# Two-layer MLP chain with banded attention: the norm's factors taken by token and spread by DMA, and a planner that shakes its due times at random

## The chip, the cores and the metric

One core of one Trainium2 chip runs the whole program. The metric is device microseconds of one execution; the times shown are medians of runs, and the profile is that of one execution.

## What is computed

The program chains three blocks. All arrays are fp32.

```python
scores = scale * q @ k.T + bias, kept where the key is global (8) or within the last 96
x1 = softmax(scores) @ v                       # (2, 8, 768, 64) -> 1536 tokens x 512
x2 = np.maximum(x1 @ w_in, 0.0) ** 2 @ w_out   # 512 -> 2048 -> 512
rms = np.sqrt(np.mean(x2 * x2, axis=-1, keepdims=True) + 1e-06)
xn = x2 / rms * rms_g
out = (silu(xn @ w_gate) * (xn @ w_val)) @ w_out2   # 512 -> 1536 -> 512
```

## The kernel before

Tokens are cut into four chunks `c` of 384 columns. Activations lie transposed: features on the 128 partitions, tokens along the row, in tiles `xh`, `xl` (a high and a low part of each fp32 number). A product of two such split operands is three matmuls (`mm3`, lines 385 to 387) into one PSUM bank `b0` to `b7`.

The stages follow each other on TensorE (PE):
- **Attention** for the four chunks (tiles `ps`, `p`, `tb`, `pt`, `av`), with the first four of the sixteen feature blocks of the first MLP for chunks 0 to 2 laid between (`first`). Weights come by DMA into `wraw` and are unpacked on ACT (L416, L418), DVE (L420), and split into `M` (L375, L376).
- **First MLP**, middle blocks: `squared` and `outs`, a seven-product scheme over pairs of chunks (`quad`), sums into `y`.
- **First MLP, last four blocks, and the norm** (`rest`, `norm_sum`, `norm`): after chunk c's last `first`, ACT squares its four `y` rows, DVE adds them into `ns`, one matmul with a matrix of ones (L610) sums over the partitions and leaves the sum in all 128 rows, ACT takes the root (L613), and DVE takes the reciprocal in three pieces of 128 columns (L616). `norm` multiplies `y` by this `ns` and by `rms_g` (`fin`, L637), subtracts pairs of blocks, and splits the results into `xh`, `xl` and `ar`.
- **Second MLP**: `gated` (gate products, SiLU, value products) and `final`, which writes the output.

The order of all of this is not written by hand. `Plan` holds every operation with its engine, an assumed duration, and its dependences; `forward` plays a list schedule in which each engine takes the ready operation with the earliest due time, `backward` derives new due times from the result, and `solve` repeats this for seven values of a lead that attention gets, and keeps the due times with the earliest end. The program is then emitted in order of planned start, and every engine executes its instructions in that order. Where PE would stand idle in the plan between 1 and 60 us, or between 330 and 400 us, `emit` puts small matmuls with ones (L1362, *fillers* below) whose result nobody reads.

The planner's costs for a transfer are these: it holds SP for 0.45 us or more (`DMA`), and an operation on another engine that needs it may start 2.6 us after that (`LAT["SP"]`); an operation on the same engine that needs it may start at once, since `SAME["SP"]` is 0.

Of the kernel before, what the change touches and what calls it, by code (L numbers as in the profile page):

```python
# [3 lines left out]

# [1 line left out]

# [6 lines left out]
F32 = mybir.dt.float32  # L13
# [6 lines left out]
P = 128  # L20
# [56 lines left out]
class Plan:  # L77
# [33 lines left out]
    def solve(self):  # L111
        for o in reversed(self.ops):
            for q in o.succ:
                o.due = min(o.due, q.due - o.dur - (o.lat if q.eng != o.eng else SAME[o.eng]))
        best = None
        for lead in LEADS:
            if best is not None:
                for o, due in zip(self.ops, best[1]):
                    o.due = due - (lead if o in self.ahead else 0.0)
            for _ in range(ROUNDS):  # L120
                self.forward()
                end = max(o.end for o in self.ops)
# [146 lines left out]
class Mlp:  # L269
# [5 lines left out]

    def __init__(self, nc, plan, tl, main, late, psm, psl, srcs, gcol, epst, ones, ident, out):
        self.nc, self.plan, self.tl, self.out = nc, plan, tl, out
        self.gcol, self.epst, self.ones, self.ident, self.srcs = gcol, epst, ones, ident, srcs  # L280
        for k in range(KD):
# [8 lines left out]
        for n in range(2):  # L290
            tl.define(f"wraw{n}", main, [P, 1026], I32)
            tl.define(f"p5{n}", late, [P, CH], F32)
            tl.define(f"ns{n}", late, [P, CH], F32)
        for n in range(3):
            tl.define(f"wbits{n}", main, [P, 512], F32)
            tl.define(f"H{n}", late, [P, 512], F32R)
        for n in range(5):
            tl.define(f"ra{n}", main if n < 3 else late, [P, CH], F32)
        for n in range(4):
            tl.define(f"nq{n}", late, [P, CH], F32)  # L300
        tl.define("ar", late, [P, 24 * CH], F32R)
        for n in range(8):
            tl.define(f"b{n}", psm if n < 4 else psl, [P, 512], F32)
        self.nraw = self.nbits = self.nload = self.nact = self.nra = self.np5 = self.nnq = 0
# [234 lines left out]
            self.relu2(lambda f=f: self.tl(f"b{banks[f]}")[:, :CH], [("b", banks[f])], act[f, c % 2])  # L539
        return act  # L540

    def outs(self, f0, cs, act):
        nc = self.nc
        for c in cs:
            for e in range(KD):
                bank = e % 2
                ps = lambda bank=bank: self.tl(f"b{bank}")[:, :CH]
                y, ry = (lambda e=e, c=c: self.y(e, c)), self.yres(e, c)
                for f in range(2):
                    w, rw = self.w[("out", f0 + f), e]  # L550
                    self.mm3(bank, w, act[f, c % 2][0], f == 0, f == 1, CH, rw + self.both(act[f, c % 2][1]))
                self.op("DVE", DVE(CH), lambda y=y, ps=ps: nc.vector.tensor_tensor(  # L552
                    out=y(), in0=ps(), in1=y(), op=ALU.add), [("b", bank)] + ry, ry)
                yield
# [41 lines left out]
    def norm_sum(self, c, bank):  # L596
# [3 lines left out]
        for e in range(KD):  # L600
# [5 lines left out]
            t, rt = (lambda n=n: tl(f"nq{n}")), [("nq", n)]  # L606
            self.op("ACT", ACT(CH), lambda e=e, t=t: nc.scalar.activation(t(), self.y(e, c), AF.Square), self.yres(e, c), rt)
            self.op("DVE", DVE(CH), lambda t=t: nc.vector.tensor_tensor(out=s(), in0=s(), in1=t(), op=ALU.add), rs + rt, rs, port=True)
        ps = lambda: tl(f"b{bank}")[:, :CH]
        self.op("PE", 0.75, lambda: nc.tensor.matmul(  # L610
            ps(), lhsT=self.ones, rhs=s(), start=True, stop=True, skip_group_check=True), rs, [("b", bank)],
            due=self.clock - (12.0 if bank == 7 else 0.0), mode="full", slack=NSLACK)
        self.op("ACT", ACT(CH) + 1.3, lambda: nc.scalar.activation(  # L613
            s(), ps(), AF.Sqrt, bias=self.epst, scale=1.0 / DM), [("b", bank)], rs)
        for i in range(NT):
            self.op("DVE", 0.85, lambda i=i: nc.vector.reciprocal(  # L616
                s()[:, i * P : (i + 1) * P], s()[:, i * P : (i + 1) * P]), rs, rs)

    def norm(self, p):

# [681 lines left out]
def kernel(  # L1302
# [23 lines left out]
    with ExitStack() as cx:  # L1326
        cx.enter_context(tc.manual_schedule(engines=None))
        plan, tl = Plan(), Lazy()
        main, psm = Late(tc, cx, "main"), Late(tc, cx, "psm", **space)
        late, psl = Late(tc, cx, "late"), Late(tc, cx, "psl", **space)  # L1330
        main(), psm()
        ax = ExitStack()
        ap, psa = Late(tc, ax, "attn"), Late(tc, ax, "psa", **space)
        ap(), psa()
        mlp = Mlp(nc, plan, tl, main, late, psm, psl, srcs, gcol, epst, ones, ident, out)
        fetch, count, nl, ng = scalars(nc, const, counts)
        att = Attention(nc, plan, tl, ap, psa, mlp, kq, vab, ident, nl, ng)
        plan.add("ACT", 0.45, fetch, (), ["nw"], due=0.0, lat=LAT["SP"])
# [26 lines left out]
    with tc.If(said["value"] < 1):  # L1365
        with ExitStack() as cx:
            plan, tl = Plan(), Lazy()
            main, psm = Late(tc, cx, "gmain"), Late(tc, cx, "gpsm", **space)
            main()
            late = Late(tc, cx, "glate")  # L1370
            mlp = Mlp(nc, plan, tl, main, late, psm, psm, srcs, gcol, epst, ones, ident, out)
            general_attention(tc, kq, vab, nl, ng, ident, mlp)
            for c in range(NC_ - 1):
                mlp.begin(c, None)
            mlp.rest(mlp.clock)
            plan.solve().emit()
# [62 lines left out]
```

## Time and profile before

| what | value |
|---|---|
| median of 3 runs | 637.46 us (635.98 to 637.98) |
| the profiled execution | 636.76 us |
| its span, first to last instruction | 635.0 us |
| mean granted TensorE clock | 0.999 |
| PE busy (matmuls), PE weight loads busy | 624.0 us, 591.7 us |
| DVE, ACT, POOL busy | 454.4, 421.7, 158.9 us |
| DMA traffic | 56.34 MB, mean 89 GB/s |

The page counts an engine as busy while an instruction is in it. A matmul's record is its whole passage through the array: a 384-column matmul is recorded with 345 ns although the next one starts some 173 ns later, so the records overlap, and short pauses of PE hide under them. Pauses of PE are therefore read here from the starts of successive matmuls.

### The profile page before, as it was taken

The page shows a single profiled execution, that of the slowest core. Times are in us where ns is not written, and L with a number is a line of the kernel's source. Part 1 is how long each engine was busy: PE and PEld are TensorE (multiplying, and loading weights), DVE is VectorE, ACT ScalarE, POOL GpSimd, SP SyncE. Part 2 cuts the span into 40 slices and gives each one's busy share as a digit, 9 for nine tenths or more (in the row PEclk, how much of TensorE's full clock was granted, in tenths as well). Part 3 has the DMA queues.
Part 4 walks back from the last instruction along what each step waited for, and adds up shares of the span by engine and source line. Part 5 has one row for each costly group of instructions (what it writes and reads, how often), then busy time and mean ns, then how long its engine had stood idle before and what let it go on. Part 6 is the DMA issues. An engine that isn't in the chain of part 4 may idle for free.

```text
span 635.0 us, 10497 instructions
## 1 busy us (share of the span) xinstructions
PE 624.0 (98%) x3740; PEld 591.7 (93%) x3740; DVE 454.4 (72%) x1007; ACT 421.7 (66%) x954; POOL 158.9 (25%) x235
## 2 busy tenths in 40 slices
PE   8899999999999999999999999999999999999996
PEld 8789899999999999999999989999999998999995
DVE  6777989859998777785569998458458458546444
ACT  5899797958977887775659877846445445453310
POOL 6442455332404300042001204221232133140000
PEclk9999999999999999999999999999999999999999
DMA  7875767101224244233000111423213114010023
GB/s 238 231 233 156 202 163 192 42 12 66 67 67 129 71 133 133 66 105 97 0 1 1 67 35 34 132 67 100 67 35 123 43 34 133 33 35 2 0 91 114
DMA packets 20845, 56.34 MB, mean 89 GB/s; under 512 B 3248, under 2 KB 6064, under 8 KB 20784
## 3 DMA queue, kind: packets, MB, share of 16 engines
q1 hardware_dynamic: 19472, 53.82, 27.9%
q10 hardware_dynamic: 1312, 1.77, 0.8%
q8 instruction: 31, 0.51, 0.3%
q14 instruction: 30, 0.25, 0.1%
HBM read 52.43 MB, written 3.15 MB: 88 GB/s over the span
## 4 chain that ended last, share of the span: by engine, by line
PE 88%; DVE 4%; ACT 4%; DMA 2%; issue 1%; POOL 1%; POOLq 0%; ACTq 0%; DVEq 0%
PE b L386 26%; PE b L385 26%; PE b L387 26%; PE tb L1065 2%; PE av L1075 2%; PE ps L1026 2%; PE b L1362 1%; DMA wraw<-in_w_in_dram 1%; ACT p L1048 1%; PE ps L1034 1%; DVE p L1044 1%; DMA wraw<-in_w_out_dram 1%; DVE ns L616 0%; DVE wbits L420 0%; DVE qs L983 0%
## 5 line engine op out<-in xcount | busy, mean ns | idle before, releaser
L385 PE MATMUL b<-xh,M 128*128 128x384 f32 x384 | 132.3, 345 | 0.2 <-ACT ra L481 0.2
L387 PE MATMUL b<-xh,M 128*128 128x384 f32 x384 | 129.1, 336 | 0.0
L386 PE MATMUL b<-xl,M 128*128 128x384 f32 x384 | 129.1, 336 | 0.0
L376 POOL TENSOR_TENSOR M<-wbits,M 128x512 fp32r<-128x512 f32 x32 | 47.2, 1480 | 158.2 <-ACT M L375 158.1
L385 PEld LDWEIGHTS b<-xh,M 128*128 128x128 f32 x384 | 72.2, 188 | 2.5 <-ACT ra L481 0.6
L386 PEld LDWEIGHTS b<-xl,M 128*128 128x128 f32 x384 | 72.1, 188 | 2.1 <-DVE xl L376 0.3
L387 PEld LDWEIGHTS b<-xh,M 128*128 128x128 f32 x384 | 72.1, 188 | 0.2
L385 PE MATMUL b<-h,M 128*128 128x384 f32 x208 | 71.7, 345 | 0.0
L386 PE MATMUL b<-h,M 128*128 128x384 f32 x208 | 70.0, 337 | 0.1
L387 PE MATMUL b<-h,M 128*128 128x384 f32 x208 | 69.7, 335 | 0.0
L742 DVE TENSOR_TENSOR y<-b,y 128x512 f32<-128x512 f32 (+1 forms) x61 | 41.6, 682 | 37.2 <-PE b L387 36.2
L375 ACT CAST M<-wbits 128x512 fp32r<-128x512 f32 x81 | 49.9, 621 | 19.5 <-PE b L387 9.9
L420 DVE SCALAR_TENSOR_TENSOR wbits<-wraw,wbits 128x512 int32<-128x512 int32 x68 | 47.3, 695 | 16.4 <-ACT wbits L418 12.6
L456 POOL TENSOR_TENSOR wbits<-wbits 128x256 f32<-128x256 f32 x16 | 13.3, 833 | 174.9 <-DVE wbits L420 174.9
L386 PE MATMUL b<-M,h 128*128 128x512 f32 (+1 forms) x146 | 56.9, 390 | 0.0
L385 PE MATMUL b<-M,h 128*128 128x512 f32 (+1 forms) x146 | 56.8, 389 | 0.0
L387 PE MATMUL b<-M,h 128*128 128x512 f32 (+1 forms) x146 | 56.8, 389 | 0.0
L1048 ACT ACTIVATE p<-p,few 128x256 f32<-128x256 f32 (+1 forms) x96 | 46.9, 497 | 12.5 <-DVE few L1044 8.7
L416 ACT ACTIVATE wbits<-wraw 128x512 f16<-128x512 bf16 x68 | 45.2, 668 | 11.9 <-POOL wbits L456 5.8
L484 DVE TENSOR_TENSOR h<-ra,h 128x384 fp32r<-128x384 f32 x64 | 39.3, 618 | 13.0 <-ACT ra L483 12.6
L552 DVE TENSOR_TENSOR y<-b,y 128x384 f32<-128x384 f32 x64 | 34.6, 551 | 13.5 <-PE b L387 13.5
L709 ACT ACTIVATE ra<-b 128x384 f32<-128x384 f32 x36 | 17.6, 491 | 39.9 <-PE b L387 39.9
(145 smaller groups left out, 1540.7 us busy)
## 6 DMA issues: line engine op xcount, KB each, us to landing
wraw<-in_w_out_dram SPq DMA_DIRECT2D x28, 512.0 KB, 3.4
wraw<-in_w_in_dram SPq DMA_DIRECT2D x16, 512.0 KB, 4.1
wraw<-in_w_gate_dram SPq DMA_DIRECT2D x12, 512.0 KB, 3.3
wraw<-in_w_val_dram SPq DMA_DIRECT2D x12, 512.0 KB, 3.3
raw<-in_kq_dram SPq DMA_DIRECT2D x16, 240.0 KB, 4.7
raw<-in_kq_dram SPq DMA_DIRECT2D x16, 208.0 KB, 4.8
v<-in_vab_dram SPq DMA_DIRECT2D x8, 384.0 KB, 3.1
v<-in_vab_dram SPq DMA_DIRECT2D x8, 256.0 KB, 3.5
```

Source lines behind the costliest of these rows:

```text
L375: self.op("ACT", ACT(n), lambda: nc.scalar.copy(dst()[0], src()), rs, [(x, "hi") for x in ws])
L376: self.op(eng, t(n), lambda: e.tensor_tensor(out=dst()[1], in0=src(), in1=f32(dst()[0]), op=ALU.subtract), rs + [(x, "hi") for x in ws], [ ...
L385: nc.tensor.matmul(ps, lhsT=wh, rhs=ah, start=first, stop=False, skip_group_check=True)
L386: nc.tensor.matmul(ps, lhsT=wh, rhs=al, start=False, stop=False, skip_group_check=True)
L387: nc.tensor.matmul(ps, lhsT=wl, rhs=ah, start=False, stop=last, skip_group_check=True)
L416: self.plan.add("ACT", ACT(512), lambda: nc.scalar.activation(tl(bits)[:, 256:].bitcast(F16), head(), AF.Copy), rr, rb)
L420: self.plan.add("DVE", DVE(512), lambda: nc.vector.scalar_tensor_tensor(out=bi(), in0=tail(), scalar=13, in1=bi(), op0=ALU.logical_shift_r ...
L484: self.op("DVE", DVE(CH), lambda: nc.vector.tensor_tensor(out=get()[1], in0=t(), in1=f32(get()[0]), op=ALU.subtract), rt + hi, lo, port=True)
L552: self.op("DVE", DVE(CH), lambda y=y, ps=ps: nc.vector.tensor_tensor(out=y(), in0=ps(), in1=y(), op=ALU.add), [("b", bank)] + ry, ry)
L709: self.op("ACT", ACT(CH), lambda: nc.scalar.activation(t(), src(), AF.Silu), rs, rt)
L742: self.op("DVE", DVE(a1 - a0), lambda o=o, ps=ps: nc.vector.tensor_tensor(out=o(), in0=ps(), in1=o(), op=ALU.add), [("b", bank)] + ro, ro)
L1048: self.op("ACT", 0.29 + w / 1200, lambda j=j: nc.scalar.activation(tl(f"p{m}")[:, j, :w], tl(f"p{m}")[:, j, :w], AF.Exp, bias=tl("few")[:, ...
```

## The change

There are three parts. `norm_sum` no longer has the sums in all rows: three matmuls with `ns` as the stationary operand and one column of ones give one sum per token, in three columns of a PSUM bank; the root and the reciprocal are taken on 128 x 3 numbers (`rt`); then one DMA writes these 384 numbers into a row in DRAM (`far`), and a second DMA reads that row back into all 128 partitions of `ns`. `solve` goes on, after its rounds, with 56 shakes: each draws, from a listed seed, a moment, a width and a strength, moves the due times of the operations planned around that moment by random amounts, and keeps the result if a score (planned end plus 0.3 of the mean end of PE's operations) got smaller. And `outs` gets an argument `on`, by which ACT would carry `y` through the bank; every caller leaves it at its default `()`.

```diff
+SHAKES = (
+    200006, 200011, 200013, 200014, 200015, 200022, 200026, 200031, 200032, 200034, 200035, 200037, 200042, 200045,
...
+)
...
         for o, due in zip(self.ops, best[1]):
             o.due = due
+        self.forward()
+        self.best = None
+        self.better([o.due for o in self.ops])
+        for n in SHAKES:
+            self.shake(n)
+        for o, (due, _) in zip(self.ops, self.best[1]):
+            o.due = due
         return self.forward()
+
+    def better(self, dues):
+
+        pe = [o.end for o in self.ops if o.eng == "PE"]
+        score = max(o.end for o in self.ops) + 0.3 * sum(pe) / len(pe)
+        if self.best and score >= self.best[0] - 1.0e-6:
+            return score < self.best[0] + 1.0
+        self.best = (score, [(due, o.start) for due, o in zip(dues, self.ops)])
+        return True
+
+    def shake(self, n):
+
+        draw = Random(n)
+        at, width, by = draw.uniform(0.0, 640.0), draw.choice((5.0, 15.0, 40.0)), draw.choice((0.5, 1.5, 4.0))
+        for o, (due, start) in zip(self.ops, self.best[1]):
+            o.due = due + (draw.gauss(0.0, by) if abs(start - at) < width else 0.0)
+        for _ in range(3):
+            dues = [o.due for o in self.ops]
+            if not self.forward().better(dues):
+                break
+            self.backward()
...
+            tl.define(f"rt{n}", late, [P, NT], F32)
...
+        for n in range(NC_):
+            tl.define(f"far{n}", far, [1, CH], F32)
...
-        ps = lambda: tl(f"b{bank}")[:, :CH]
-        self.op("PE", 0.75, lambda: nc.tensor.matmul(
-            ps(), lhsT=self.ones, rhs=s(), start=True, stop=True, skip_group_check=True), rs, [("b", bank)],
-            due=self.clock - (12.0 if bank == 7 else 0.0), mode="full", slack=NSLACK)
-        self.op("ACT", ACT(CH) + 1.3, lambda: nc.scalar.activation(
-            s(), ps(), AF.Sqrt, bias=self.epst, scale=1.0 / DM), [("b", bank)], rs)
-        for i in range(NT):
-            self.op("DVE", 0.85, lambda i=i: nc.vector.reciprocal(
-                s()[:, i * P : (i + 1) * P], s()[:, i * P : (i + 1) * P]), rs, rs)
+        ps, r, rr = (lambda: tl(f"b{bank}")[:, :NT]), (lambda: tl(f"rt{c % 2}")), [("rt", c % 2)]
+        far, rf = (lambda: tl(f"far{c}")), [("far", c)]
+
+        def sums():
+            for i in range(NT):
+                nc.tensor.matmul(ps()[:, i : i + 1], lhsT=s().rearrange("p (n i) -> p i n", i=NT)[:, i], rhs=self.ones[:, :1],
+                                 start=True, stop=True, skip_group_check=True)
+        self.op("PE", 0.25 * NT, sums, rs, [("b", bank)], due=self.clock - (12.0 if bank == 7 else 0.0), mode="full", slack=NSLACK)
+        self.op("ACT", ACT(NT) + 1.4, lambda: nc.scalar.activation(
+            r(), ps(), AF.Sqrt, bias=self.epst, scale=1.0 / DM), [("b", bank)], rr)
+        self.op("DVE", 0.16, lambda: nc.vector.reciprocal(r(), r()), rr, rr)
+        self.op("SP", 0.1, lambda: nc.sync.dma_start(
+            out=far().rearrange("a (p i) -> (a p) i", i=NT), in_=r()), rr, rf)
+        self.op("SP", DMA(192), lambda: nc.sync.dma_start(out=s(), in_=far().broadcast_to([P, CH])), rf, rs)
```

The built programs show how this moves instructions. Over the whole program PE gets 12 narrow matmuls for 4 wide ones and 32 fillers for 38 (before, 33 stood ahead of the first weights and 5 in the norm; now all 32 stand ahead of the first weights); DVE gets 4 reciprocals for 12; SP gets 8 transfers. Nearly every engine's order differs in small exchanges. Three places follow, as the order of each program lists them: operation, tiles written and read (with buffer numbers), shape, and the semaphores waited for.

SP's queue around the norm, before (`wraw` are the raw weights of the second MLP):

```order
L415 DMA wraw0_194<-in_w_gate_dram 128x2048 [waits DMAHW6_49,DVE_49]
L415 DMA wraw0_194<-in_w_val_dram 128x2048 [waits DMAHW0_49,DVE_49]
L415 DMA wraw1_244<-in_w_gate_dram 128x2048 [waits DMAHW7_49,DVE_49]
L415 DMA wraw1_244<-in_w_val_dram 128x2048 [waits DMAHW2_49,DVE_49,Activation_49]
L415 DMA wraw0_194<-in_w_out2_dram 128x2048 [waits DMAHW1_49,DVE_49]
```

And now:

```order
L453 DMA wraw0_192<-in_w_val_dram 128x2048 [waits DMAHW0_49,DVE_49]
L664 DMA far0_3363<-rt0_3345 128x3 [waits DVE_49,PE_49,Pool_49]
L666 DMA ns0_1814<-far0_3363 128x384 [waits DMAHW2_49,PE_49]
L664 DMA far1_3470<-rt1_3449 128x3 [waits DVE_49]
L666 DMA ns1_1778<-far1_3470 128x384 [waits DMAHW4_49,PE_49]
L453 DMA wraw1_229<-in_w_gate_dram 128x2048 [waits DMAHW7_49,DVE_49]
L664 DMA far2_3701<-rt0_3345 128x3 [waits DVE_49]
L666 DMA ns0_1814<-far2_3701 128x384 [waits DMAHW7_49,PE_49]
L453 DMA wraw1_229<-in_w_val_dram 128x2048 [waits DMAHW6_49,DMAHW1_49,DVE_49]
L664 DMA far3_3799<-rt1_3449 128x3 [waits DVE_49]
L666 DMA ns1_1778<-far3_3799 128x384 [waits DMAHW3_49,DMAHW2_49,PE_49]
```

The read-back of each chunk stands directly behind its write and waits for the write's own semaphore; three weight loads stand behind such pairs.

DVE's order at the norm of chunk 3, before (`ns` the norm's factors, `ra` and `h` the activation of the second MLP on its way, `nq` the normed rows):

```order
L616 RECIPROCAL ns_1816<-ns_1816 128x128 [waits Activation_49]
L678 TENSOR_TENSOR b_105<-b_456,p_2071 128x384 [waits PE_49]
L616 RECIPROCAL ns_1816<-ns_1816 128x128
L713 TENSOR_TENSOR ra_1843<-b_1870,ra_1843 128x384 [waits PE_49]
L616 RECIPROCAL ns_1816<-ns_1816 128x128
L420 SCALAR_TENSOR_TENSOR wbits_398<-wraw_194,wbits_398 128x512 [waits DMAHW1_49,Activation_49,Pool_49]
L713 TENSOR_TENSOR ra_631<-b_105,ra_631 128x384 [waits PE_49]
L688 TENSOR_TENSOR ra_1868<-b_456,p_2071 128x384 [waits PE_49]
L637 SCALAR_TENSOR_TENSOR nq_1779<-y_102,gcol,ns_1816 128x384 [waits DVE_49]
L713 TENSOR_TENSOR ra_616<-ra_1868,ra_616 128x384 [waits DVE_49]
L376 TENSOR_TENSOR h_623<-ra_631,h_623 128x384 [waits Activation_49]
```

And now:

```order
L663 RECIPROCAL rt_3449<-rt_3449 128x3 [waits Activation_49]
L727 TENSOR_TENSOR b_109<-b_455,p_2085 128x384 [waits PE_49]
L762 TENSOR_TENSOR ra_1831<-b_1864,ra_1831 128x384 [waits PE_49]
L458 SCALAR_TENSOR_TENSOR wbits_401<-wraw_192,wbits_401 128x512 [waits DMAHW1_49,Activation_49,Pool_49]
L762 TENSOR_TENSOR ra_634<-b_109,ra_634 128x384 [waits PE_49]
L737 TENSOR_TENSOR ra_1861<-b_455,p_2085 128x384 [waits PE_49]
L686 SCALAR_TENSOR_TENSOR nq_1789<-y_89,gcol,ns_1778 128x384 [waits DMAHW3_49]
L762 TENSOR_TENSOR ra_627<-ra_1861,ra_627 128x384 [waits DVE_49]
L414 TENSOR_TENSOR h_642<-ra_634,h_642 128x384 [waits Activation_49]
```

The first use of the factors (L637, now L686) waited for DVE itself and now waits for a transfer; behind it on DVE stands the low part of `h`, the stationary operand of the first product of `final`.

ACT's order in the first 30 us, before (`wbits` a weight being unpacked, `xh` the attention's result, `pt` the transposed probabilities that PE needs next):

```order
L1067 COPY pt1_255<-tb_221 128x512 [waits PE_49]
L1048 ACTIVATE p1_187,few_175<-p1_187,few_175 128x128 [waits DVE_49,Pool_49] x2
L416 ACTIVATE wbits2_398<-wraw0_194 128x512 [waits DMAHW6_49]
L375 CAST xh1_82<-av_289 128x384 [waits PE_49]
L1067 COPY pt2_277<-tb_221 128x2x128 [waits PE_49]
```

And now:

```order
L1097 ACTIVATE p1_187,few_174<-p1_187,few_174 128x128 [waits DVE_49,Pool_49]
L1097 ACTIVATE p1_187,few_174<-p1_187,few_174 128x128 [waits DVE_49]
L413 CAST M1_389<-wbits1_310 128x512 [waits DVE_49]
L413 CAST xh1_82<-av_294 128x384 [waits PE_49]
L454 ACTIVATE wbits2_401<-wraw0_192 128x512 [waits DMAHW6_49]
L1116 COPY pt2_277<-tb_221 128x2x128 [waits PE_49]
```

The instruction that waits for the third weight transfer stands behind two casts now instead of ahead of one of them.

## Rows read from the trace of the kernel before

**Rows 1.** The page, part 1: busy us, share of the span, instructions of each engine.

```profile
PE 624.0 (98%) x3740; PEld 591.7 (93%) x3740; DVE 454.4 (72%) x1007; ACT 421.7 (66%) x954; POOL 158.9 (25%) x235
```

**Rows 2.** Stretches: length, busy us by engine (instructions), PE clock, DMA share, GB/s.

```profile
0.00:30.00 30.00, 26.36 (x191) 23.43 (x191) 20.73 (x91) 20.11 (x63) 16.11 (x45) 1.00 0.82 232
30.00:140.00 110.00, 109.61 (x891) 101.10 (x889) 89.19 (x309) 95.18 (x280) 46.07 (x98) 1.00 0.54 148
140.00:340.00 200.00, 199.63 (x1146) 198.18 (x1143) 157.48 (x283) 150.65 (x308) 36.63 (x33) 1.00 0.23 74
340.00:380.00 40.00, 39.57 (x214) 36.73 (x213) 38.39 (x72) 32.90 (x67) 4.53 (x5) 1.00 0.12 41
380.00:620.00 240.00, 240.00 (x1263) 224.91 (x1262) 142.43 (x245) 121.93 (x240) 55.54 (x55) 1.00 0.19 62
```

**Rows 3.** Timeline of PE: start, us, line, tiles, shape, count [idle before].

```profile
358.33 0.81 PE L610 MATMUL b<-ns,ones 128*128 128x384 f32 x2
...
359.15 0.33 PE L386 MATMUL b<-xl,M 128*128 128x384 f32 x1
...
365.58 0.34 PE L387 MATMUL b<-xh,M 128*128 128x384 f32 x1
366.33 0.94 PE L1362 MATMUL b<-ones 128*128 128x128 f32 x6 [0.41 <-DVE ra L713]
367.02 0.43 PE L385 MATMUL b<-ar,H 128*128 128x384 f32 x1
...
368.15 0.38 PE L1362 MATMUL b<-ones 128*128 128x128 f32 x2
...
371.15 0.38 PE L1362 MATMUL b<-ones 128*128 128x128 f32 x2
```

**Rows 4.** Timeline of PE in the first 30 us.

```profile
26.11 1.03 PE L1026 MATMUL ps<-k,raw 128*128 128x256 f32 x4
28.66 0.66 PE L1065 MATMUL tb<-ident,p 128*128 128x128 f32 x4 [1.52 <-ACT pt L1067]
```

**Rows 5.** Timeline of ACT in the same stretch.

```profile
27.32 0.65 ACT L416 ACTIVATE wbits<-wraw 128x512 f16<-128x512 bf16 x1 [2.08 <-DMA wraw<-in_w_in_dram]
27.88 0.46 ACT L375 CAST xh<-av 128x384 fp32r<-128x384 f32 x1
28.23 0.37 ACT L1067 COPY pt<-tb 128x256 f32<-128x256 f32 x1
```

**Rows 6.** The chain that ended last, in order of time: start, us, what, count.

```profile
31.22 0.44 PE tb L1065 x4
...
33.05 1.24 PE av L1075 x20
```

**Rows 7.** Groups of instructions by shape: count, busy us, mean ns, idle before.

```profile
L616 DVE RECIPROCAL ns<-ns 128x128 f32<-128x128 f32 x12 | 11.1, 935 | 1.6 <-ACT ns L613 1.6
...
L1055 DVE RECIPROCAL few<-few 128x2 f32<-128x2 f32 x48 | 7.8, 162 | 7.6 <-POOL few L1052 6.9
```

**Rows 8.** Timeline of ACT at the norm of chunk 3.

```profile
360.52 0.58 ACT L613 ACTIVATE ns<-b,epst 128x384 f32<-128x384 f32 x1
```

**Rows 9.** Timeline of DVE at the norm of chunk 3.

```profile
363.72 0.94 DVE L616 RECIPROCAL ns<-ns 128x128 f32<-128x128 f32 x1
...
366.66 0.61 DVE L637 SCALAR_TENSOR_TENSOR nq<-y,gcol,ns 128x384 f32<-128x384 f32 x1
367.18 0.55 DVE L713 TENSOR_TENSOR ra<-ra,ra 128x384 f32<-128x384 f32 x1
```

**Rows 10.** DMA issues: transfer, count, KB each, median us to landing.

```profile
wraw<-in_w_gate_dram SPq DMA_DIRECT2D x12, 512.0 KB, 3.3
...
out_dram<-y SPq DMA_DIRECT2D x6, 256.0 KB, 2.0
...
q<-in_kq_dram SPq DMA_DIRECT2D x6, 96.0 KB, 4.6
...
gcol<-in_rms_g_dram SPq DMA_DIRECT2D x1, 2.0 KB, 4.7
```

More of the change, by code (lines that the diff above doesn't have):

```diff
@@ L3 @@
 from heapq import heappop, heappush
+from random import Random
 import numpy as np
@@ L269, with __init__ @@
 class Mlp:
-    def __init__(self, nc, plan, tl, main, late, psm, psl, srcs, gcol, epst, ones, ident, out):
+    def __init__(self, nc, plan, tl, main, late, far, psm, psl, srcs, gcol, epst, ones, ident, out):
         self.nc, self.plan, self.tl, self.out = nc, plan, tl, out
@@ L540, in plain, with outs @@
         return act
-    def outs(self, f0, cs, act):
+    def outs(self, f0, cs, act, on=()):
         nc = self.nc
@@ L548, in outs @@
                 y, ry = (lambda e=e, c=c: self.y(e, c)), self.yres(e, c)
+                if e in on:
+                    self.op("ACT", ACT(CH), lambda y=y, ps=ps: nc.scalar.copy(ps(), y()), ry, [("b", bank)])
                 for f in range(2):
                     w, rw = self.w[("out", f0 + f), e]
-                    self.mm3(bank, w, act[f, c % 2][0], f == 0, f == 1, CH, rw + self.both(act[f, c % 2][1]))
+                    self.mm3(bank, w, act[f, c % 2][0], f == 0 and e not in on, f == 1, CH, rw + self.both(act[f, c % 2][1]))
+                if e in on:
+                    self.op("ACT", ACT(CH), lambda y=y, ps=ps: nc.scalar.copy(y(), ps()), [("b", bank)], ry)
+                    yield
+                    continue
                 self.op("DVE", DVE(CH), lambda y=y, ps=ps: nc.vector.tensor_tensor(
@@ L1330 @@
         late, psl = Late(tc, cx, "late"), Late(tc, cx, "psl", **space)
+        far = Late(tc, cx, "far", space=bass.MemoryType.DRAM)
         main(), psm()
@@ L1334 @@
         ap(), psa()
-        mlp = Mlp(nc, plan, tl, main, late, psm, psl, srcs, gcol, epst, ones, ident, out)
+        mlp = Mlp(nc, plan, tl, main, late, far, psm, psl, srcs, gcol, epst, ones, ident, out)
         fetch, count, nl, ng = scalars(nc, const, counts)
@@ L1370 @@
             late = Late(tc, cx, "glate")
-            mlp = Mlp(nc, plan, tl, main, late, psm, psm, srcs, gcol, epst, ones, ident, out)
+            far = Late(tc, cx, "gfar", space=bass.MemoryType.DRAM)
+            mlp = Mlp(nc, plan, tl, main, late, far, psm, psm, srcs, gcol, epst, ones, ident, out)
             general_attention(tc, kq, vab, nl, ng, ident, mlp)
```

3 rows, old and new, of the table SHAKES are left out of this document.

## The prediction

> **What bounds the kernel now.** I read the shares of busy time first, then stretches, then the starts of PE's matmuls, and only then the waits of the other engines.
>
> PE is the bound over nearly the whole span: its matmuls cover 98% [rows 1]. By stretches it is covered fully from 380 to 620 us, and lacks 0.39 us between 30 and 140 and 0.37 us between 140 and 340 [rows 2]. Between 140 and 340 us 1146 matmuls fill 200 us, 0.174 us each; that is the pace of a 384-column product. Since recorded passages overlap, a pause shorter than a passage doesn't show in the busy time, so I looked at starts. What is left for a better order are three kinds of place:
>
> - The first 30 us. PE waits for transfers and for the first attention tiles and fills with ones. One pause there is the program's own making: PE waits 1.52 us for the copy of `pt` [rows 4]; ACT had been stuck for 2.08 us on the third weight transfer, then made a cast, then the copy at 28.23 us [rows 5].
> - The norm, 340 to 380 us, where DVE is busy 38.39 of 40 us [rows 2]. From the product at 365.58 (plus its 0.17) to the next real one at 367.02 PE loses 1.27 us, with six records of fillers in it; two more fillers stand at 368.15 and 371.15 [rows 3]. A filler costs two records of 0.115 us (six in 0.69 us), so the two are 0.46 us, and the stretch loses 1.7 us in all.
> - Scattered short pauses, at most some 0.8 us between 30 and 340 us by the stretches above.
>
> The tail after the last product isn't touched. So everything that an order could win is about 1.7 + 1.5 + 0.8 = 4.0 us, plus what the start's fillers hide, while any new wait of PE is paid in full.
>
> **The change, part by part.** The sum is made against the profiled execution, 636.76 us, which lies 0.70 us under the median of 637.46; the difference found is then put to the median.
>
> *The sums on PE: 0.* A wide sum costs 0.65 us: from 358.33 to the second product behind it at 359.15, less one product of 0.17 [rows 3]. The narrow ones aren't in the trace. They have one moving column but 128 stationary ones. Two rows tell which of them sets the pace: `tb` has 128 stationary and 128 moving columns and takes 0.44/4 = 0.11 us a record, `av` has 64 stationary and 128 moving and takes 1.24/20 = 0.062 [rows 6]. The pace follows the stationary side, so three fp32 matmuls of two records are 6 x 0.11 = 0.66 us. Four times 0.01 us is nothing. If only moving columns counted it would be up to -2.4 us in all; if the step of three between stationary columns doubled the load, +2.6 us. I take 0, from the nearest row.
>
> *Reciprocals on DVE: 11.1 us gone, 4 x 0.16 us come* [rows 7]. Half of them stood in the full stretch of DVE, so DVE gets some 5 us of air there. By itself this is worth nothing on PE but the 1.7 us that PE lost.
>
> *The round trip.* Before, the sum of chunk 3 ends at 358.98, the root at 361.10 (2.1 us later) and the last reciprocal at 364.66: the factors are there 5.7 us after the sum [rows 3, 8, 9]. Now it is 2.1 for the root (its three columns may save a little of 0.58), 0.3 for the reciprocal with its handoff, and then two transfers, the second issued when the first has landed. The trace has no such pair. From below: two transfers as quick as the output's 2.0 us, 4.0; from above: two like `q` and `gcol`, 4.6 + 4.7 = 9.3 [rows 10]. Those two belong to the first 30 us, where the transfer engines are busy 82% of the time; at the norm it is 12% [rows 2], so I stay near the quick end: 2.0 for the write, and 2.3 for the read, which at 192 KB lies between the output's 256 KB at 2.0 and the gate weights' 512 KB at 3.3. That makes T = 4.3, and the factors 6.7 us after the sum, 1.0 us later than before. The `gcol` row also says that small pieces cost little: its 4-byte pieces landed in 4.7 us beside `q`'s 4.6.
>
> The Trainium skill speaks against this step. "DMA: Bandwidth & Descriptors", section "Anatomy of one DMA — SWDGE (gpsimd) path", gives each transfer a fixed 2.0 us, most of it the receipt from the target memory, plus bytes at 436 GB/s. By it the pair would be 4.45 us, an estimate of that page, and the sum below 0.3 us worse; the output's row with 2.0 us for 256 KB is quicker than the page's 2.6.
>
> Who waits for it? The planner books 0.1 us for the write, lets the read go at once (same engine, 0), 0.72 for the read and 2.6 to its user: 3.4 us, so DVE's order has the first use where 3.4 would suit, and T is 0.9 more. Behind that use on DVE stand two instructions up to the low part of `h`, which `final`'s first product needs. From the sum to that product PE's order has 48 products, 48 x 0.174 = 8.4 us. The chain needs 2.4 + T + three instructions of about 0.5 (one takes from 366.66 to 367.18 [rows 9]) + 0.3 of handoffs = 4.2 + T. It is even at T = 4.2; at 4.3 PE waits 0.1 us. The same test for chunk 1: from its sum to the next product that needs DVE's work behind the first use there are 108 products, 18.8 us, and 25 instructions of some 0.48 us on DVE, so 2.4 + T + 12.0 + 0.3: even at 4.1, a wait of 0.2. Chunks 0 and 2 have other DVE work of more than T in front. So the norm's loss of 1.7 us becomes 0.3: **-1.4 us** (-1.7 at T = 4.0; nothing gained at T = 5.0). SP's weight loads behind the pairs are those of the second pair of weight blocks and later; the cover is the whole first gate and value product.
>
> *The start.* ACT now makes two casts ahead of the transfer's wait, so the copy of `pt` follows directly: 28.23 against 27.88, 0.35 us earlier, and another half microsecond of ACT's work lies inside the 2.08 us wait. One filler fewer is planned. I take **-0.6 us** (0 if the transfer lands later, since the transfers of `v` and `q` ahead of it were reordered too; -1.5 if the pause goes).
>
> *All other exchanges:* of 0.8 us between 30 and 340 half may go: **-0.4 us**, with -0.8 and +0.8 as bounds, since a random exchange is judged by planned durations and may open as many pauses as it closes. `outs` with `on` changes nothing.
>
> Sum: 0 - 1.4 - 0.6 - 0.4 = -2.4 us: 634.4 us for an execution like the profiled one, **635.1 us** as a median.
>
> **The rivals.**
> 1. *The round trip holds DVE, and DVE holds PE (slower).* For it: the factors' first use stands in DVE's queue ahead of PE's next operands, twice with a slack near zero, and the planner doesn't know that the read waits for the write. Against: quiet transfer engines. Beyond 4.1 each 1 us of T costs twice 1 us. The gains without it are -2.7 us, so the kernel is slower by 0.3% (1.9 us, about what a measurement can tell from no change) from T = 6.4 on; at T = 7 it is +3.1 us, 640.6.
> 2. *The shakes cure what only the plan has (same).* For it: PE's real pauses outside the start and the norm are small, and the plan's durations differ from the chip's. Then start and exchanges give nothing and the norm, with T near 4.6, -0.9 us: 636.6.
> 3. *More comes (faster still).* The narrow sums overlap with their neighbours (-1.5) and the start's pause goes (-1.5) beside the norm's -1.4 and -0.4: -4.8 us, 632.7. For it: fillers fell from 38 to 32. Against: the weight load sets the pace of narrow matmuls.
>
> **How the numbers follow.** Forecast 0.42, rival 3 0.1, rival 2 0.36, rival 1 0.12. The forecast lies at -0.37%, just past the bound of 0.3%, so it and rival 3 are the 0.52 for faster. The range goes from rival 3 with a little of its tail cut, 632.2, to the lower part of rival 1, 638.8 (T = 6.1).
>
> **What would show it.** Right: no fillers and no pause over 0.3 us between 360 and 380 us; a reciprocal of some 0.16 us; write and read landing in about 2.0 and 2.3 us; narrow sums of about 0.66 us; ACT's copy directly behind the unpacking near 28 us. Wrong: DVE idle for several microseconds ahead of L686, released by a transfer, with PE idle behind it; or new pauses of PE between 30 and 340 us.

## The result and the profile after

| | time, us | ratio to before |
|---|---|---|
| before, beside the changed kernel | 637.66, median of 7 (635.98 to 638.74) | |
| changed kernel | 642.76, median of 7 (639.88 to 645.21) | 1.0083 (95%: 1.0056 to 1.0109) |
| changed kernel once more, with the experiments | 642.83, median of 5 (642.05 to 643.99) | 1.0091 (1.0076 to 1.0106) |

The kernel became slower by about 5.3 us (0.8 to 0.9%; the medians differ by 5.1 and 5.5 us from those of the runs beside them); forecast were 635.1 us and a gain. The profiled execution took 642.73 us, its span is 640.9 us against 635.0.

Stretches of the changed kernel, columns as in [rows 2]:

```profile
0.00:30.00 30.00, 26.74 (x193) 23.95 (x194) 20.79 (x96) 21.02 (x65) 16.43 (x47) 1.00 0.87 234
30.00:140.00 110.00, 108.69 (x881) 99.85 (x881) 88.72 (x304) 94.18 (x277) 47.17 (x96) 1.00 0.56 148
140.00:340.00 200.00, 199.20 (x1146) 196.97 (x1143) 152.11 (x271) 144.90 (x302) 35.42 (x32) 1.00 0.25 76
340.00:380.00 40.00, 37.66 (x197) 35.11 (x196) 31.23 (x64) 29.89 (x61) 7.18 (x6) 0.96 0.20 50
380.00:620.00 240.00, 240.00 (x1262) 224.54 (x1261) 146.22 (x249) 124.15 (x248) 54.84 (x55) 1.00 0.18 60
```

The norm, 340 to 380 us, stands out: DVE has 7 us less to do there (31.23 for 38.39 busy), and PE lost by it: 37.66 for 39.57, and the granted clock is 0.96. DVE was relieved, as meant; it then waited for the factors: 2.53 us for those of chunk 1, 1.05 for chunk 2's, 2.27 for chunk 3's. Its timeline at the norm of chunk 3 (start, us, what, idle before and its releaser), with the first line from chunk 1:

```profile
332.54 1.15 DVE L686 SCALAR_TENSOR_TENSOR nq<-y,gcol,ns 128x384 f32<-128x384 f32 x2 [2.53 <-DMA ns<-far]
...
364.60 0.17 DVE L663 RECIPROCAL rt<-rt 128x3 f32<-128x3 f32 x1 [0.16 <-ACT rt L661]
...
369.16 0.55 DVE L737 TENSOR_TENSOR ra<-b,p 128x384 f32<-128x384 f32 x1
371.98 0.62 DVE L686 SCALAR_TENSOR_TENSOR nq<-y,gcol,ns 128x384 f32<-128x384 f32 x1 [2.27 <-DMA ns<-far]
372.52 0.55 DVE L762 TENSOR_TENSOR ra<-ra,ra 128x384 f32<-128x384 f32 x1
372.99 0.55 DVE L414 TENSOR_TENSOR h<-ra,h 128x384 fp32r<-128x384 f32 x1
```

The reciprocal takes 0.17 us where three took 2.8 [rows 7]. But from its end, 364.77, to the first use of the factors, 371.98, lie 7.2 us, and the low part of `h`, which needs no norm, stands two places behind that use. SP's two issues, and then PE's timeline:

```profile
364.80 0.32 SPq L664 DMA_DIRECT2D far<-rt  x1
367.00 0.32 SPq L666 DMA_DIRECT2D ns<-far  x1
```

```profile
371.16 0.40 PE L424 MATMUL b<-M,h 128*128 128x512 f32 x1
373.59 0.50 PE L425 MATMUL b<-M,h 128*128 128x512 f32 x1 [2.03 <-DVE h L414]
373.93 0.53 PE L423 MATMUL b<-M,h 128*128 128x512 f32 x1
374.26 0.63 PE L424 MATMUL b<-M,h 128*128 128x512 f32 x1
```

PE waits 2.03 us for that `h`, and the products after it run at the lower of the two clock levels, 1.2 GHz: this stretch of 4 us has a granted clock of 0.57, so 3.4 us of it at half speed:

```profile
374.00:378.00 4.00, 4.00 (x13) 3.19 (x12) 4.00 (x10) 2.31 (x5) 0.00 (x0) 0.57 0.00 0
```

The transfers (KB each, median us to landing), to be set beside [rows 10]:

```profile
ns<-far SPq DMA_DIRECT2D x4, 192.0 KB, 4.3
...
far<-rt SPq DMA_DIRECT2D x4, 1.5 KB, 2.1
```

The write is as forecast; the read takes 4.3 us instead of 2.3. That is the median of four; they run from 4.1 to 5.0, and chunk 3 has the 5.0 (issued at 367.00, its data used at 371.98). And a narrow sum on PE, here that of chunk 2:

```profile
350.42 0.34 PE L425 MATMUL b<-h,ar 128*128 128x384 f32 x1
350.60 1.04 PE L658 MATMUL b<-ones,ns 128*128 128x1 f32 x6
351.50 0.42 PE L423 MATMUL b<-h,ar 128*128 128x384 f32 x1
351.76 0.37 PE L424 MATMUL b<-h,ar 128*128 128x384 f32 x1
```

Measured as the wide one was, from its first record to the second product behind it less one product, it costs 351.76 - 350.60 - 0.17 = 0.99 us, against 0.65 [rows 3].

**Where the 5.9 us of the two spans lie.** For each stretch I took its length less what its matmuls need at their undisturbed spacing (0.173 us for 384 columns, 0.229 for 512, 0.120 for 256, 0.111 for 128; about 0.21 for the 256 columns of scores from unsplit operands and 0.06 for `av`; a sum 0.64 wide, 0.67 narrow), so fillers, pauses and low clock count as lost. One execution each:

| PE's lost time, us | 0-30 | 30-140 | 140-300 | 300-340 | 340-380 | 380-end | sum |
|---|---|---|---|---|---|---|---|
| before | 13.95 | 3.88 | 1.60 | -0.10 | 2.41 | 8.06 | 29.8 |
| changed | 13.26 | 4.95 | 3.14 | 0.72 | 5.79 | 7.82 | 35.7 |
| changed, once more | 14.55 | 5.10 | 3.07 | 0.89 | 3.32 | 8.19 | 35.1 |
| e1, norm alone | 13.43 | 3.88 | 1.43 | 0.72 | 8.10 | 8.08 | 35.6 |
| e2, shakes alone | 14.77 | 4.89 | 3.07 | 0.07 | 1.95 | 8.73 | 33.5 |
| e3, no trip | 13.60 | 4.23 | 2.99 | 0.72 | 1.68 | 9.32 | 32.5 |
| e7, priced | 13.60 | 4.06 | 1.43 | 0.72 | 2.54 | 8.20 | 30.6 |
| e10, priced, shaken | 12.00 | 3.93 | 1.43 | 0.89 | 2.02 | 8.35 | 28.6 |

Between the two executions of the changed kernel the first column differs by 1.3 us and the norm's by 2.5, the others by 0.1 to 0.4; e3, in the same order, has 0.7 to 0.9 us less than they at 30 to 140 us. The columns of 140 to 340 us hardly vary. Against before, the changed kernel loses 1.5 us at 140 to 300 (no norm there: the new order), 0.8 at 300 to 340 (two narrow sums), and 3.4 in the norm in one execution, 0.9 in the other.

### The profile page after: what moved, and what is told of

It reads as the page before. It is cut to its first block, busy times and chain, and to the rows that moved or that the text cites. A ratio compares the mean times of both kernels' runs of the same rounds, so it can differ in the third digit from the quotient of the medians.

```text
span 640.9 us, 10487 instructions
## 1 busy us (share of the span) xinstructions
PE 627.3 (98%) x3744; PEld 593.5 (93%) x3744; DVE 449.8 (70%) x999; ACT 416.2 (65%) x954; POOL 161.0 (25%) x235
## 4 chain that ended last, share of the span: by engine, by line
PE 74%; DVE 13%; ACT 7%; DMA 4%; issue 1%; POOL 0%; DVEq 0%; ACTq 0%; SPq 0%
PE b L424 22%; PE b L423 22%; PE b L425 22%; ACT p L1097 2%; PE av L1124 2%; PE tb L1114 2%; DMA ns<-far 1%; PE ps L1083 1%; DVE h L522 1%; DVE wbits L458 1%; DMA wraw<-in_w_out_dram 1%; DVE ar L414 1%; PE b L1412 1%; DVE y L596 1%; DMA wraw<-in_w_in_dram 1%
## 5 line engine op out<-in xcount | busy, mean ns | idle before, releaser
L791 DVE TENSOR_TENSOR y<-b,y 128x512 f32<-128x512 f32 (+1 forms) x61 | 41.5, 682 | 33.7 <-PE b L425 33.5
L425 PE MATMUL b<-M,h 128*128 128x512 f32 (+1 forms) x146 | 57.4, 393 | 2.0 <-DVE h L414 2.0
L424 PE MATMUL b<-M,h 128*128 128x512 f32 (+1 forms) x146 | 57.7, 395 | 0.0
L423 PE MATMUL b<-M,h 128*128 128x512 f32 (+1 forms) x146 | 57.3, 393 | 0.0
L413 ACT CAST h<-ra 128x384 fp32r<-128x384 f32 x48 | 24.3, 512 | 40.5 <-DVE ra L762 40.0
L424 PE MATMUL b<-ar,M 128*128 128x384 f32 x128 | 43.3, 338 | 0.0
```

Of the source, the lines that this page charges most:

```text
L413: self.op("ACT", ACT(n), lambda: nc.scalar.copy(dst()[0], src()), rs, [(x, "hi") for x in ws])
L423: nc.tensor.matmul(ps, lhsT=wh, rhs=ah, start=first, stop=False, skip_group_check=True)
L424: nc.tensor.matmul(ps, lhsT=wh, rhs=al, start=False, stop=False, skip_group_check=True)
L425: nc.tensor.matmul(ps, lhsT=wl, rhs=ah, start=False, stop=last, skip_group_check=True)
L791: self.op("DVE", DVE(a1 - a0), lambda o=o, ps=ps: nc.vector.tensor_tensor(out=o(), in0=ps(), in1=o(), op=ALU.add), [("b", bank)] + ro, ro)
```

## The experiments

**The yardstick.** The changed kernel unaltered, beside the next three.

> The changed kernel once more, as the yardstick for the runs beside it. Every theory: about 642.8 us, between 640 and 645; DVE waits 2 to 2.6 us for the read at the third factor use, PE 2.0 to 2.2 us behind it near 371 us, and the granted clock of 370 to 380 us is about 0.83.

642.83 us, as before, but not by the same sum. Here the read of chunk 3 was issued at 368.36 us and its data used at 372.45, 4.1 us on instead of 5.0, and PE's wait for `h` was 1.13 us, with no low clock behind it (370 to 380 us at 1.00). Instead 3.4 us of low clock lay near 30 us (28 to 34 us at 0.72), behind a wait of 1.94 us for `pt`:

```profile
28.97 0.65 PE L1114 MATMUL tb<-ident,p 128*128 128x128 f32 x4 [1.94 <-ACT pt L1116]
...
374.06 0.50 PE L425 MATMUL b<-M,h 128*128 128x512 f32 x1 [1.13 <-DVE h L414]
```

So the expected 0.83 wasn't there: the place and size of the loss differ between executions, the clock's share above all.

**e1: the norm alone.**

```diff
-SHAKES = (
...
-)
+SHAKES = ()
```

> The norm by token, no shakes. Round-trip theory: the read's 4.3 us are the same, so PE pauses about 2 us near 371 us and the clock falls after it: 640 to 641 us, that is 2 to 3 us over the kernel before. Shakes theory (the random exchanges opened the pauses): no worse than the kernel before, 636 to 637.5 us.

644.05 us, 1.0109 (1.0094 to 1.0124): no better than the changed kernel, so the loss doesn't need the shakes. In its trace PE waits twice in the norm, here and ahead of 371.55 (1.21 us), and the clock is down again:

```profile
369.55 0.45 PE L418 MATMUL b<-xh,M 128*128 128x384 f32 x1 [2.12 <-DVE ra L757]
```

```profile
370.00:375.00 5.00, 3.79 (x17) 3.47 (x16) 3.84 (x9) 2.51 (x6) 0.00 (x0) 0.66 0.34 105
```

**e3: the same order without the trip.** Both entries on SP stay in the plan and issue nothing, so the scaling takes the sums of squares themselves.

```diff
-        self.op("SP", 0.1, lambda: nc.sync.dma_start(
-            out=far().rearrange("a (p i) -> (a p) i", i=NT), in_=r()), rr, rf)
-        self.op("SP", DMA(192), lambda: nc.sync.dma_start(out=s(), in_=far().broadcast_to([P, CH])), rf, rs)
+        self.op("SP", 0.1, lambda: None, rr, rf)
+        self.op("SP", DMA(192), lambda: None, rf, rs)
```

> The changed kernel in its very order, but the write and the read of the factors are left out, so the scaling uses the sums of squares themselves. Round-trip theory: the 2.2 us pause of PE at 371 us and the 1.7 us of low clock behind it go: 4 us less than the changed kernel, about 638.8 us; what stays over the kernel before (1 us or so) is the shakes'. Shakes theory: within 0.8 us of the changed kernel, about 642 us. If more than 5 us go, the trip costs in other places too.

640.56 us, 1.0050 (1.0036 to 1.0064): the trip costs the changed kernel 2.3 us, not the 4 that I read from one profile (that execution had the longer pause and the clock's fall). The norm's loss falls to 1.68 us in the table. 3.2 us over the kernel before remain, more than the shakes were meant to explain: that made me measure the sums.

**e4: fillers in the pause.**

```diff
         plan.solve()
+        plan.fill += 8 * [mlp.gap.start]
```

(`mlp.gap` is the first product of `final`.)

> The changed kernel with 8 filler products (1.84 us) put into PE's order just ahead of the pause at 371 us. If the pause is what lowers the clock: granted clock of 370 to 380 us near 1.0 and 1.6 us less than the changed kernel, about 641.2 us. If the low clock has another cause: 370 to 380 us stays at about 0.83 and the time within 0.6 us of the changed kernel's.

641.68 us, 1.0076 (1.0062 to 1.0091), 1.15 us less than the yardstick, though the two intervals overlap. PE's timeline at the place:

```profile
369.50 1.95 PE L1414 MATMUL b<-ones 128*128 128x128 f32 x16
...
372.19 0.50 PE L425 MATMUL b<-M,h 128*128 128x512 f32 x1 [0.27 <-DVE h L414]
```

The granted clock of 370 to 380 us is 1.00. One trace can't tell, since the yardstick's has 1.00 there too; but over the whole span all five executions of e4 have a granted clock of 0.997 to 0.999, those of the yardstick 0.994 to 0.999, and those of e1 0.993 to 0.995. So a pause can be paid twice, itself and by the clock after it, and work of no use in the pause probably wins back the second part; the times alone don't show it. It is less than the 1.6 us expected, as it must be if some executions of the changed kernel don't pay it.

**e2: the shakes alone**, on the kernel before (the planner's part of the diff, `norm_sum` as it was).

> The kernel before with the shakes alone (wide sums, reciprocals on DVE, no transfers). If random exchanges open as much as they close on the chip: within 1 us of the kernel before, 636.5 to 638.5 us, with new pauses of PE between 140 and 300 us. If they really cure: under 636 us. If they are what made the changed kernel slow: 640 us or more.

638.94 us, 1.0033 (1.0019 to 1.0047): 1.65 us lost, past the 1 us expected of "open as much as they close". The table has 1.5 us of it at 140 to 300 us, the same as in the changed kernel. There its stretches read

```profile
140.00:200.00 60.00, 59.35 (x350) 57.17 (x349) 57.11 (x102) 48.36 (x105) 14.86 (x13) 1.00 0.22 71
200.00:300.00 100.00, 99.81 (x575) 99.49 (x574) 73.23 (x128) 73.62 (x149) 20.55 (x20) 1.00 0.31 97
```

and those of e10 below, whose plan is shaken too:

```profile
140.00:200.00 60.00, 59.62 (x341) 58.80 (x340) 59.12 (x106) 51.19 (x110) 18.14 (x15) 1.00 0.23 71
200.00:300.00 100.00, 100.00 (x578) 100.00 (x577) 70.76 (x128) 73.90 (x150) 16.45 (x17) 1.00 0.33 104
```

575 matmuls in 100 us against 578 is a pause of half a microsecond.

**e5: neighbouring columns.**

```diff
-lhsT=s().rearrange("p (n i) -> p i n", i=NT)[:, i]
+lhsT=s()[:, i * P : (i + 1) * P]
-out=far().rearrange("a (p i) -> (a p) i", i=NT), in_=r()
+out=far().rearrange("a (i p) -> (a p) i", p=P), in_=r()
```

> The changed kernel with each narrow sum over 128 neighbouring columns; the write then lands in 4-byte pieces. If the step of three between stationary columns is what makes a narrow sum cost 0.99 us: 6 records of 0.11 us, 0.66 us a sum, 1.3 us less in all, about 641.4 us. If a narrow product of this kind costs 0.17 us a record in any case: 0.99 us a sum as before and 642.8 us. The write of 4-byte pieces: 2.1 us to landing if pieces cost little, over 3 us if each piece counts.

672.22 us, 1.0552 (1.0537 to 1.0566). The sums did what the step theory said (0.11 us a record; one of the four fell into low clock). The write didn't:

```profile
far<-rt SPq DMA_DIRECT2D x4, 1.5 KB, 8.2
```

384 pieces of 4 bytes instead of 128 of 12 take 6.1 us longer to land. In the prediction I had excused small pieces by `gcol` [rows 10]; that one reads them, this one writes them. Unmeant, the run shows how the trip acts: 6.1 us more on it, four times, cost 29 us. PE has five pauses of 2.0 to 7.7 us, 26 us together by the starts of its matmuls, and the granted clock from 320 to 410 us is 0.83, which is some 30 us at the lower level, in part within these pauses.

**e7: the trip rightly priced**, no shakes.

```diff
-        self.op("PE", 0.25 * NT, sums, rs, [("b", bank)], due=self.clock - (12.0 if bank == 7 else 0.0), mode="full", slack=NSLACK)
+        self.op("PE", 0.33 * NT, sums, rs, [("b", bank)], due=self.clock - (12.0 if bank == 7 else 0.0), mode="full", slack=NSLACK)
...
-        self.op("SP", DMA(192), lambda: nc.sync.dma_start(out=s(), in_=far().broadcast_to([P, CH])), rf, rs)
+        self.op("SP", DMA(192), lambda: nc.sync.dma_start(out=s(), in_=far().broadcast_to([P, CH])), rf, rs, lat=5.9)
```

> The norm by token without shakes, but the planner is told the trip's true length (6.6 us in place of 3.4 from the write's issue) and the sums' 0.99 us. To be held against the norm alone (644.05 us). If the wrong price is what put the wait in PE's way: the pause near 365 to 372 us shrinks to under 1 us and the time falls by 2 to 4 us, 640 to 642 us. If the chain is too long for any order: pause and time stay, 643.5 to 644.5 us.

637.46 us, 1.0005 (0.9996 to 1.0014): 6.6 us less than e1, by two numbers in the planner, which weren't tried apart; more than the 2 to 4 expected. DVE's timeline at the norm of chunk 3 now reads

```profile
361.25 0.18 DVE L658 RECIPROCAL rt<-rt 128x3 f32<-128x3 f32 x1 [0.53 <-ACT rt L656]
...
368.14 0.56 DVE L757 TENSOR_TENSOR ra<-ra,ra 128x384 f32<-128x384 f32 x1
368.62 0.55 DVE L409 TENSOR_TENSOR h<-ra,h 128x384 fp32r<-128x384 f32 x1
369.08 0.61 DVE L681 SCALAR_TENSOR_TENSOR nq<-y,gcol,ns 128x384 f32<-128x384 f32 x1
```

The use of the factors comes 7.6 us after the reciprocal, and DVE waits for none of the reads: the two instructions for `h` that stood behind it stand in front. The chain was never too long; it was put in the wrong place.

**e8: no transfers, no reciprocals**, root and reciprocals as two passes on ACT.

```diff
-            s(), ps(), AF.Sqrt, bias=self.epst, scale=1.0 / DM), [("b", bank)], rs)
-        for i in range(NT):
-            self.op("DVE", 0.85, lambda i=i: nc.vector.reciprocal(
-                s()[:, i * P : (i + 1) * P], s()[:, i * P : (i + 1) * P]), rs, rs)
+            s(), ps(), AF.Ln, bias=self.epst, scale=1.0 / DM), [("b", bank)], rs)
+        self.op("ACT", ACT(CH) + 1.3, lambda: nc.scalar.activation(s(), s(), AF.Exp, scale=-0.5), rs, rs)
```

> The kernel before, with the root and the three reciprocals replaced by two passes on ACT over the 384 columns: a logarithm, then an exponential of minus one half of it. No transfers, no shakes. If DVE's reciprocals are what cost PE its 1.7 us in the norm: those go nearly all, about 636 us. If ACT's two table loads per norm take their place (some 1.3 us each, ACT being busy three quarters there): PE pauses behind ACT and the time is 638 us or more.

640.32 us, 1.0043 (1.0030 to 1.0057): the time foreseen for the case of the table loads. ACT's timeline at the norm of chunk 3 has a load for each function and a third to go back:

```profile
361.22 1.28 ACT L613 ACT_TABLE_LOAD   x1
...
363.48 1.28 ACT L615 ACT_TABLE_LOAD   x1
...
365.32 1.28 ACT L707 ACT_TABLE_LOAD   x1
```

The kernel before has two of these three already, one ahead of the root and one to go back:

```profile
359.23 1.28 ACT L613 ACT_TABLE_LOAD   x1
...
361.12 1.28 ACT L709 ACT_TABLE_LOAD   x1
```

So what is new there is one load and the second pass. By the count of the table PE loses 3.5 us from 340 to 380 us, for 2.4 before: 1.1 of the 3.0 us. The rest lies in other stretches of a new order, and no run shows what makes it.

**e6: what the read's time is made of.**

```diff
+            if c == 0:
+                nc.sync.dma_start(out=s(), in_=self.kq[0, 0][:, KW : KW + CH])
+            elif c == 1:
+                for h in range(2):
+                    part = slice(h * P // 2, (h + 1) * P // 2)
+                    nc.sync.dma_start(out=s()[part], in_=far().broadcast_to([P // 2, CH]))
+            elif c == 2:
+                nc.sync.dma_start(out=s()[:4], in_=far().broadcast_to([4, CH]))
+            else:
+                nc.sync.dma_start(out=s(), in_=far().broadcast_to([P, CH]))
```

> The changed kernel with another read behind the write in three of the four chunks: chunk 0 reads 128 different rows of an input instead of one row 128 times, chunk 1 the one row by two transfers of 64 partitions, chunk 2 the row into 4 partitions alone (6 KB); chunk 3 is unchanged. The factors of chunks 0 and 2 are then not the norm's. If reading one row for all partitions is what makes the read slow: chunk 0 lands in about 2.3 us, chunk 3 in 4.3. If any read of DRAM is that slow (the input's reads of 64 and 96 KB took 3.4 and 4.2): chunk 0 about 4 us, and chunk 2 hardly less than 3.4. If its size counts: chunk 2 well under 3 us.

```profile
ns<-in_kq_dram SPq DMA_DIRECT2D x1, 192.0 KB, 5.0
ns<-far SPq DMA_DIRECT2D x2, 96.0 KB, 3.4
ns<-far SPq DMA_DIRECT2D x1, 192.0 KB, 4.8
```

The one execution took 643.24 us. 128 different rows took 5.0 us, one row 128 times 4.8: reading the same row isn't the cause, a read of 192 KB takes about that long here. These are single transfers, and the one of 5.0 was in flight with the write, for which it doesn't wait. Halves of it took 3.4, so size counts for something. The 6 KB read has no landing in the trace, so the fixed part stays open.

**e9: priced, neighbouring columns, DVE reads the factors with a step** (`out` and `in0` are cut into the same three blocks, which leaves their order as it was; the sums are priced at 0.22 us a column here and in e11 and e12).

```diff
-lhsT=s().rearrange("p (n i) -> p i n", i=NT)[:, i]
+lhsT=s()[:, i * P : (i + 1) * P]
-in1=tl(f"ns{c % 2}")
+in1=tl(f"ns{c % 2}").rearrange("p (n i) -> p i n", i=NT)
```

> The rightly priced kernel without shakes (637.46 us), with narrow sums over neighbouring columns (0.67 us each where they stood 0.99) and the write still in 12-byte pieces; the factors then lie in another order, and the 16 scalings on DVE read them with a step of three. If the sums and the trip are the whole story: 4 x 0.32 = 1.3 us less, about 636.2 us, a little faster than the kernel before. If DVE's stepped read costs (a scaling well over 0.5 us): the norm's pauses come back, 637.5 us or more.

639.70 us, 1.0034 (1.0021 to 1.0047). The sum of chunk 2, by the same measure, costs 351.80 - 350.95 - 0.17 = 0.68 us:

```profile
350.95 0.72 PE L653 MATMUL b<-ones,ns 128*128 128x1 f32 x6
351.54 0.42 PE L418 MATMUL b<-h,ar 128*128 128x384 f32 x1
351.80 0.34 PE L419 MATMUL b<-h,ar 128*128 128x384 f32 x1
```

But the step has moved to DVE. Its 16 scalings, in e7 and then in e9 (busy us, mean ns):

```profile
L681 DVE SCALAR_TENSOR_TENSOR nq<-y,gcol,ns 128x384 f32<-128x384 f32 x16 | 9.9, 630 | 0.1
```

```profile
L682 DVE SCALAR_TENSOR_TENSOR nq<-y,gcol,ns 128x384 f32<-128x384 f32 x16 | 11.6, 749 | 0.1
```

1.3 us won on PE, 1.7 us more on DVE in the stretch where PE waits for it, and 2.2 us lost in the whole. By the count of the table its norm, 340 to 380 us, loses 4.3 us, where e7's loses 2.5. Why it costs more than DVE's added time isn't settled.

**e10: e7 with the list of shakes.**

> The rightly priced kernel (637.46 us without shakes) with the list of shakes put back. If the shakes open pauses on the chip that the plan doesn't see, as they did alone: 638.5 to 639.5 us, with 1 us or more of new pauses between 140 and 300 us. If they only hurt by moving the norm: within 0.6 us of 637.46. If they cure: 636 us.

636.59 us, 0.9990 (0.9978 to 1.0003), 0.9 us less than e7, which the overlapping intervals don't quite tell from no difference, and no new pauses at 140 to 300 us. So it isn't a rule that shakes open pauses; on this plan the accepted ones don't. It is the lowest time found, and not measurably faster than the kernel before.

**e11 and e12: the step in ACT's squares**, on e7 and on e10.

```diff
+        def square(t, e):
+            if c < 2:
+                nc.scalar.activation(t.rearrange("p (i n) -> p n i", i=NT), self.y(e, c).rearrange("p (n i) -> p n i", i=NT), AF.Square)
+            else:
+                nc.scalar.activation(t.rearrange("p (i n) -> p i n", i=NT), self.y(e, c).rearrange("p (n i) -> p i n", i=NT), AF.Square)
...
-lhsT=s().rearrange("p (n i) -> p i n", i=NT)[:, i]
+lhsT=s()[:, i * P : (i + 1) * P]
```

> The rightly priced kernel without shakes (637.46 us), where ACT's squares leave the tokens in three blocks (chunks 0 and 1 by a stepped write, 2 and 3 by a stepped read), so the sums take neighbouring columns, and write, read and scalings stay as they were. If ACT's steps are free: sums of 0.67 us, 1.3 us less, about 636.2 us. If they cost as DVE's did (0.26 us each, 16 squares): ACT gets 4 us more work in a stretch where it is busy 85%, half or all of the gain goes, 636.8 to 638 us.

> The same with the list of shakes. If what they gave on the priced plan (0.9 us) stands by itself: 0.9 us under the run beside it, about 635.3 us, faster than the kernel before by 0.3%. If a list of seeds that fits one plan is chance on another: anywhere from 1 us less to 1.7 us more than the run beside it.

639.46 us, 1.0029 (1.0017 to 1.0041), and 639.92 us, 1.0039 (1.0021 to 1.0056). The sums cost 0.67 us, but a square that took 0.52 us in e7 takes (ns, min, median, max):

```profile
L642 ACT ACTIVATE nq<-y x6: 900/908/930, 296.2 to 318.1; 128x384 f32<-128x384 f32 x6
...
L644 ACT ACTIVATE nq<-y x6: 721/723/730, 345.5 to 355.7; 128x384 f32<-128x384 f32 x6
```

0.91 us with a stepped write, 0.72 with a stepped read. e11 lies past both cases expected of it (636.2, and 636.8 to 638), so the squares' price is at most part of the 2 us over e7; the rest wasn't traced. And the same seeds that went with 0.9 us less on e7 gave nothing on e11; in e12 140 to 300 us lost 3.0 us again, as in the changed kernel. The seeds are kept by the planner's durations; on the chip what they do changes with the plan.

## Why the prediction was wrong, step by step

- *The round trip: the step that failed.* Of it the prediction said "2.3 for the read, which at 192 KB lies between the output's 256 KB at 2.0 and the gate weights' 512 KB at 3.3". The output is a write to DRAM; of the reads in [rows 10] the quickest took 3.3 us, and `q`, 96 KB, took 4.6. I stayed "near the quick end" because the transfer engines were quiet; e6 has 5.0 us for 192 KB of different rows at such a time. T was 7.2 us in chunk 3 (2.1 for the write and 5.0 for the read, whose median of four is 4.3; the rest handoffs), inside the stated bounds of 4.0 to 9.3; in the next execution it was 6.3. The Trainium skill's formula ("DMA: Bandwidth & Descriptors", section "Anatomy of one DMA — SWDGE (gpsimd) path") gave 4.45 us for the pair as an estimate. That section is about transfers that GpSimd issues, and these are issued by SP; the trace has 2.1 + 4.3 = 6.4 by medians, and the measurement decides.
- *Rival 1, with a chance of 0.12, is what happened in the norm*, as described: DVE idle ahead of L686, released by a transfer, PE idle behind it. Its arithmetic doesn't hold. T of 7.2 and 6.3 us in two executions left gaps of 2.2 and 1.3 us between the starts of PE's matmuls in chunk 3, so it is even at 5.0 us there and not at 4.2; chunk 1's wait on DVE (2.5 us) cost PE nothing visible; and the clock's fall came on top in one of them, which no step had. By e3 the trip cost 2.3 us, less than half of the loss; most of the rest came from the sums and the exchanges below, so the rival had the wait right and not the whole.
- *The cause behind it* was in the prediction, as a fact without a consequence: the planner books 3.4 us where the trip takes about 7. I asked whether T fits the order given, not what the order would be with the right T. e7 answers it: no wait for the trip is left, and the time is that of the kernel before.
- *The sums: 0 forecast, +0.34 us each, 1.4 us in all, measured.* "The pace follows the stationary side" was right, 0.11 us a record, with neighbouring columns (e5, e9, e11: 0.67 to 0.68 us a sum). With a step of three it is 0.174. I had this as the upper bound ("if the step of three doubled the load") and took the row without a step. The Trainium skill has a rule that bears on it: "Advanced Engine Details and Errata", section "SBUF Cachelines", says that an access pattern needs at least two hits on a 16-byte line for full pace; columns 12 bytes apart mostly have one. The rows of PE, DVE and ACT here all agree in sign; no run here shows that the lines are the reason.
- *Exchanges: -0.4 forecast, +1.5 us measured* at 140 to 300 us, past my bound of +0.8, and 1.65 us in e2. That half the small pauses would go was a guess, and the reason why this order opens new ones on the chip stays open.
- *Start: -0.6 forecast, -0.7 in the profiled execution* (13.26 for 13.95 us lost), and by the mechanism forecast: ACT's copy follows the unpacking at 27.40 us, and PE waits 0.93 us for it instead of 1.52. In the next execution that wait was 1.94 us and the start lost 0.6 us more than before: no dependable gain.
- *Reciprocals on DVE* went as said, 0.17 us for 2.8. What that is worth by itself no run shows; nearest is e3, where without the trip the norm loses 1.68 us for 2.41, though its two sums cost 0.6 us more: some 1.4 us, for at most 1.7 in the prediction.

The measured parts, 2.3 for the trip, 1.4 for the sums and 1.5 for the order, make 5.2 of 5.3 us. The agreement is in part luck: start and attention vary by 1 us between executions, and e3 also removes some of what the norm lost before.

## What to carry to other kernels

A transfer's price is taken from rows of the same direction: here 256 KB written to DRAM landed in 2.0 us and 192 KB read from it in 4.3. Where a planner sets the order, a new operation that it underprices is paid in the place it is given, not by its own length, so before judging the operation ask what the order would be at the right price; here two corrected numbers were worth 6.6 us to the kernel without shakes, and the change itself, so priced, about nothing. A step in an access pattern has a price on every engine: moving it from PE to DVE or ACT moved the cost.

## What the runs showed of the hardware

- A read from DRAM into 128 partitions: 4.3 us for 192 KB (4.0 to 5.1 as median in the kernels), of one row for all; one read of 128 rows took 5.0, one of a single row in the same run 4.8. A write of 1.5 KB: 2.1 us in 12-byte pieces, 8.2 us in 4-byte pieces.
- A step of three fp32 elements: 0.174 for 0.111 us a record of 128 stationary columns; 0.75 for 0.63 us on DVE (one operand); on ACT 0.72 (read) and 0.91 (write) for 0.52 us.
- PE's waits of 2.03 us (changed kernel) and of 2.12 us with 1.21 us close behind it (e1) in the norm, and one of 1.94 us at 29 us (the yardstick), were each followed by 3.4 us at 1.2 GHz; a wait of 1.13 us wasn't, nor the one in e4 that products filled up to 0.27 us.
